# Pooled attention scores over 128 rows, quartered loads, an early gather and later weight halves in a fused attention, expert and Mish kernel

## The chip, the cores and the metric

The kernel runs on one core of a Trainium2 chip. The metric is device time in microseconds of one execution, the median of the runs. The core has TensorE (matmul), VectorE, ScalarE, GpSimd and SyncE (SP), which issues the kernel's direct transfers; 16 DMA engines move the data.

## The reference

Three stages follow one another; shapes are those of the kernel.

```python
# attention: 2 batches, 8 heads, 576 positions, width 64
q_d, k_d, v_d = (t.reshape(2, 8, 144, 4, 64).mean(axis=3) for t in (q, k, v))
out_up = np.repeat(softmax(q_d @ k_d.T / 8) @ v_d, 4, axis=2)
out_local = softmax(where(abs(i - j) < 4, q @ k.T / 8, -1e9)) @ v
x = (out_up + out_local) as [1152, 512]
# 8 experts, top 1, capacity 288
e = argmax(x @ w_gate); g = softmax(x @ w_gate)[e]
y = g * (relu(x @ w1[e]) @ w2[e])      # w1 512 x 1024, w2 1024 x 512, rows over capacity are 0
# dense layer with Mish; w_in and w_out are float64
h = y @ w_in                           # 512 x 2048
out = (h * tanh(log1p(exp(h)))) @ w_out
```

The pooled scores, `q_d @ k_d.T`, are the part that the change computes in another way.

## The kernel before

**Attention** runs in steps `t`. At each step one unit starts its scores (`units[t].scores()`), the unit before it takes its exponentials, the one three steps back is transposed (`turn`) and the one four steps back is multiplied by the values. A unit is a `Local` (four heads of one tile of 96 rows, with its window of 102 keys; 12 tiles, two units each) or a `Down` (two heads of one half, 72 rows, of the pooled attention of one batch; 16 units). `ORDER` fixes the sequence: six local units, six pairs of a pooled and a local one, ten pooled ones in a row (steps 18 to 27), twelve local ones. The second batch's pooled units start at step 20.

Heads stand in pairs on the 128 partitions: 64 rows are one head, 64 the other (`a` = 0 or 1). A pooled unit takes its head's 64 rows of the pooled queries `qd` and keys `kd` (L484 to L499). Ahead of its two score matmuls it issues zero matmuls (`beat(s.sc, 2)`, L328): 128 x 512 in bfloat16, whose result the scores overwrite. Pooling (`pool_qk`, L452) sums four neighbours, on VectorE by one reduction or on GpSimd by three additions; the table `sums` says at which step VectorE pools which pair, and `before(t)` what GpSimd pools.

`before(t)` (L821) also issues loads: constants at step 6 (`load_consts`), and behind them all four loads of the second batch's keys and queries (`load_qk`); at step 8 `turn_consts` (VectorE copies of the constants) and the second batch's `v4` loads with their pools; at the steps in `CLEAR` one of nine clears of the DRAM grid; expert weights from step 22 (`load_pre`, eight pieces) and four halves of the float64 weights (`load_half`). All these transfers stand in SP's queue in the order in which they are issued, together with each tile's `vt` and `vw` loads and the `up` loads.

Up to step 37 the framework orders each engine's instructions by their priorities and its own estimate of time; from then on TensorE follows the program's order (`in_order`).

**The end of attention.** Each token gets an expert and a row (`Route`: `choose`, `place`), is scaled by its gate and scattered into the grid (`send`). The first expert's rows do not wait for the last three tiles: `gather(i)` (L891) multiplies tile 9, 10 or 11 by a one-hot matrix of rows, and `grid_rows` (L901) transposes what the grid already holds; VectorE adds the two (L1079). `gather(EARLY)` (tile 9) stands at step `END` = 44; tile 10's stood just ahead of `grid_rows` and `gather(11)`, once tile 11 is placed. `place` issues as many zero matmuls ahead of its rank matmuls (L730 to L732) as `WAITS` says: 6 for tile 10, 3 for tile 11.

**Experts** (L1272 on) run in 32 steps: eight experts with 192, 192, 184, 168, 160, 152, 144 and 120 rows (`CAPS`), four steps each. A step is `first` (L1214, 16 matmul instructions) and the `second` of the step before (L1229, 16 instructions); each uses one piece of 512 KB out of a ring of eight (`RING`), and `fetch()` loads the next piece into the place that came free, four steps ahead. In the same steps the float64 weights are split into two fp32r parts: `conv_steps(c)` makes `split` of half `c-1`, `round` of half `c`, `clamp` of half `c+1` (for this kernel a look by ScalarE, L263 and L264) and loads halves up to `c + AHEAD` (L252). Halves are 512 KB; eight are loaded before the experts start, halves 28 to 31 after them.

**The dense layer** multiplies three column blocks of 384 tokens by the split weights (`up`, L1331; `out`, L1399).

Of the kernel before, what the change touches and what calls it, by code (L numbers as in the profile page):

```python
# [9 lines left out]
F32 = mybir.dt.float32  # L10
# [27 lines left out]
CLEAR = (11, 12, 13, 14, 17, 18, 19, 23, 24)  # L38
# [5 lines left out]
AHEAD = 8  # L44
# [39 lines left out]
WAITS = {10: 6, 11: 3}  # L84
# [220 lines left out]
def attention(ctx, k, pre):  # L305
# [35 lines left out]
    def load_qk(b, s0, s1):  # L341
        for which, src in ((1, io["kT"]), (0, io["qT"])):
            for h in range(2):
                out = qkt[b][which][h][:, :, s0:s1]
                nc.sync.dma_start(out=out, in_=src[b, :, 2 * h : 2 * h + 2, s0:s1])
# [101 lines left out]
    def pool_new(b):  # L447
        qd = rot.tile([128, HP, SD], F32, tag="qd", name=f"qd{b}")
        kd = rot.tile([128, HP, SD], F32, tag="kd", name=f"kd{b}")
        down[b] = (qd, kd)  # L450

    def pool_qk(b, hp, which, eng):  # L452

        d, x = down[b][which][:, hp, :], qkt[b][which][hp // 2][:, hp % 2, :]
        x = x.rearrange("p (s r) -> p s r", r=4)
        if eng is nc.vector:
            nc.vector.reduce_sum(d, x, axis=AX.X)
        else:
            nc.gpsimd.tensor_add(d, x[:, :, 0], x[:, :, 1])
            nc.gpsimd.tensor_add(d, d, x[:, :, 2])  # L460
            nc.gpsimd.tensor_add(d, d, x[:, :, 3])
        if which == 0:
            eng.tensor_scalar_mul(d, d, 1.0 / 128.0)

# [14 lines left out]
    class Down:  # L479
# [6 lines left out]
        def scores(s):  # L486
            qd, kd = down[s.b]
            s.sc = bank("sc", "dsc" + s.nm, 3)
            beat(s.sc, 2)
            for j in range(2):  # L490
                r = slice(64 * s.a, 64 * s.a + 64)
                nc.tensor.matmul(  # L492
                    s.sc[:HALF, j * SD : (j + 1) * SD],
                    qd[r, s.hp + j, s.hf * HALF : s.hf * HALF + HALF],
                    kd[r, s.hp + j, :],
                    start=(j == 0),
                    stop=(j == 1),
                    skip_group_check=True,
                )  # L499
# [322 lines left out]
    def before(t):  # L822
# [8 lines left out]
        if t == 6:  # L831
            load_consts()
            load_qk(1, 0, S)
            for hp in range(HP):
                pool_qk(1, hp, 1, gps)
        if t == 8:
            turn_consts()
            load_v4(1, 0)
# [77 lines left out]
    while t < END or ready or choosing or chosen or placing or gating:  # L916
# [30 lines left out]
        if t == END:  # L947
            xt.extend(bank("tp", f"x0{c}", 2) for c in range(2))
            gather(EARLY)
# [31 lines left out]
        if NTT - 1 in sends:  # L981
            for i in range(EARLY + 1, NTT - 1):
                gather(i)
# [105 lines left out]
def moe(ctx, k, full, pre):  # L1089
# [63 lines left out]
    with ExitStack() as c1:  # L1153
# [107 lines left out]
        load_to(AHEAD - 1)  # L1261
# [256 lines left out]
```

## Time and profile before

| what | value |
|---|---|
| median of 3 runs | 487.97 us (487.36 to 554.25) |
| the profiled execution, own time | 489.28 us |
| its span, first to last instruction | 487.5 us |
| mean granted TensorE clock | 0.993 |
| attention, experts, dense layer (by TensorE's first matmul of each) | 0 to 128, 128 to 277, 277 to 487.5 us |

The page names engines PE (TensorE matmul), PEld (TensorE weight load), DVE (VectorE), ACT (ScalarE), POOL (GpSimd) and SP. A row of the timeline gives the start, the length, the engine, the line, the operation, the tile written and read with its shape, the count of instructions put together, and in brackets the idle time before with what ended it. An fp32 matmul appears as two instructions. The lengths of matmuls contain their pipeline's end, so the time that one takes from the stream is read from the starts of its neighbours. The chain of waits is the work that ended last, followed back from the last instruction.

### The profile page before, as it was taken

Reading aid. Unit: us, or ns where it says so; the run is one execution under the profiler, and the core shown is the slowest. Engines: PE = TensorE matmul, PEld = TensorE weight load, DVE = VectorE, ACT = ScalarE, POOL = GpSimd, SP = SyncE. Lnnn points to the kernel's source line nnn. Section 1 sums busy time; section 2 is a strip of 40 time slices with the busy share of each in tenths; the row PEclk is TensorE's granted clock in tenths of the full one; section 3 lists DMA queues with packets and bytes.
Section 4 is the critical chain, followed back from the end, with each engine's and each line's share of the span. In section 5 each row is a group of like instructions: output and inputs, shape, how many; then the busy total and the mean of one; then the engine's idle time right before and its main releaser. Section 6 shows DMA issues by size and latency. Waiting matters only on the chain.

```text
span 487.5 us, 8749 instructions
## 1 busy us (share of the span) xinstructions
PE 469.3 (96%) x3136; PEld 424.1 (87%) x3151; DVE 362.8 (74%) x738; ACT 245.0 (50%) x564; POOL 169.8 (35%) x158
## 2 busy tenths in 40 slices
PE   8989999998999999999899999999999999999992
PEld 4767777887899999999899999999888999999982
DVE  2776666769888777688789069999897878687780
ACT  2534545666545555665574156546354454544441
POOL 0364730635376466787665100223320000200002
PEclk9999999999999999999999999999999999999997
DMA  8787989867399999999988130000010000100001
GB/s 243 189 280 197 286 252 336 299 216 243 130 317 287 313 305 332 316 335 289 326 291 310 63 112 0 1 0 1 1 67 1 0 1 0 67 0 1 1 2 70
DMA packets 36205, 78.96 MB, mean 162 GB/s; under 512 B 4829, under 2 KB 17853, under 8 KB 35865
## 3 DMA queue, kind: packets, MB, share of 16 engines
q1 hardware_dynamic: 34281, 73.59, 47.5%
q0 software_dynamic: 1872, 4.73, 2.8%
q8 instruction: 27, 0.44, 0.4%
q14 instruction: 25, 0.20, 0.1%
HBM read 68.26 MB, written 10.04 MB: 161 GB/s over the span
## 4 chain that ended last, share of the span: by engine, by line
PE 48%; issue 28%; DMA 10%; DVE 9%; POOL 2%; ACT 0%; SPq 0%; POOLq 0%; DVEq 0%
PE hlm L1214 11%; PE yam L1229 11%; PE h2m L1331 4%; PE sc L596 4%; DMA mw250r<-in_w 3%; DMA mw153r<-in_w 3%; DMA xgm<-grid 2%; DMA pack<-in_c_pack 2%; PE pv L644 2%; POOL out L149 2%; PE dsc L492 2%; PE dpv L532 2%; PE oam L1399 2%; PE tp L629 1%; PE sc L605 1%
## 5 line engine op out<-in xcount | busy, mean ns | idle before, releaser
L1331 PE MATMUL h2m<-mxh,mw 128*128 128x384 f32 x384 | 103.0, 338 | 0.0
L1399 PE MATMUL oam<-mw,gm 128*128 128x512 f32 x432 | 102.6, 390 | 0.0
L1399 PEld LDWEIGHTS oam<-mw,gm 128*128 128x128 f32 x432 | 80.7, 188 | 15.0
L1331 PEld LDWEIGHTS h2m<-mxh,mw 128*128 128x128 f32 x384 | 70.1, 187 | 1.1
L1331 PE MATMUL h2m<-mxl,mw 128*128 128x384 f32 x192 | 64.9, 338 | 0.0
L149 POOL DMA_INDIRECT out<-obm,tok_s x9 | 8.9, 988 | 121.6 <-ACT obm L1410 121.3
L296 POOL TENSOR_TENSOR mw_in_t<-mw_in_t 128x512 f32<-128x512 f32 x16 | 22.3, 1392 | 56.9 <-DVE mw_in_t L293 51.1
L1387 ACT CAST gm<-wtm 128x768 fp32r<-128x768 f32 (+1 forms) x26 | 20.3, 784 | 36.3 <-DVE wtm L1386 36.2
L1331 PEld LDWEIGHTS h2m<-mxl,mw 128*128 128x128 f32 x192 | 36.0, 187 | 1.0
L1381 ACT ACTIVATE um<-wtm,two 128x768 f32<-128x768 f32 (+1 forms) x26 | 23.0, 888 | 25.3 <-DVE wtm L1379 25.2
L1369 ACT ACTIVATE um<-h2m 128x768 f32<-128x768 f32 (+1 forms) x26 | 19.6, 761 | 28.8 <-PE h2m L1331 28.8
L1378 DVE TENSOR_SCALAR um<-um 128x768 f32<-128x768 f32 (+1 forms) x26 | 13.5, 526 | 25.9 <-ACT um L1369 25.9
L296 POOL TENSOR_TENSOR mw_out_t<-mw_out_t 128x512 f32<-128x512 f32 x16 | 25.1, 1567 | 18.8 <-DVE mw_out_t L293 18.8
L618 ACT ACTIVATE p<-sc,mx 96x102 f32<-96x102 f32 (+1 forms) x96 | 25.0, 340 | 13.0 <-DVE mx L612 9.1
L1384 DVE SCALAR_TENSOR_TENSOR wtm<-wtm,um 128x768 f32<-128x768 f32 (+1 forms) x26 | 23.3, 895 | 8.9 <-ACT um L1383 8.4
L1388 DVE TENSOR_TENSOR gm<-wtm,gm 128x768 fp32r<-128x768 f32 (+1 forms) x26 | 25.2, 976 | 5.7 <-ACT gm L1387 5.7
L302 POOL TENSOR_TENSOR mw<-mw_in_t,mw 128x512 fp32r<-128x512 f32 x16 | 21.5, 1345 | 19.1 <-ACT mw L301 16.3
L286 DVE TENSOR_SCALAR mw_out_t<-mr 128x512 int32<-128x512 int32 x16 | 17.5, 1091 | 13.4 <-POOL mw L302 11.0
L692 POOL TENSOR_TENSOR x<-x,up 96x512 f32<-96x512 f32 x12 | 15.2, 1270 | 35.1 <-DMA up<-up_d 13.5
L302 POOL TENSOR_TENSOR mw<-mw_out_t,mw 128x512 fp32r<-128x512 f32 x16 | 21.3, 1332 | 16.9 <-ACT mw L301 12.8
L596 PEld LDWEIGHTS sc<-kt,qt 64*96 64x96 f32 x192 | 18.3, 159 | 7.8 <-issue 7.3
L1385 DVE SCALAR_TENSOR_TENSOR um<-wtm,um 128x768 f32<-128x768 f32 (+1 forms) x26 | 24.4, 937 | 0.5
(304 smaller groups left out, 1070.9 us busy)
## 6 DMA issues: line engine op xcount, KB each, us to landing
mr<-in_w_in SPq DMA_DIRECT2D x16, 512.0 KB
mr<-in_w_out SPq DMA_DIRECT2D x16, 512.0 KB
grid<-zero SPq DMA_DIRECT2D x9, 512.0 KB
pr<-in_w SPq DMA_DIRECT2D x8, 512.0 KB
vt<-in_vt SPq DMA_DIRECT2D x12, 204.0 KB
up<-up_d SPq DMA_DIRECT2D x12, 195.0 KB
v<-in_v SPq DMA_DIRECT2D x4, 576.0 KB
vw<-in_vw SPq DMA_DIRECT2D x8, 232.7 KB
```

The source lines that it names most:

```text
L296: s.k.nc.gpsimd.tensor_add(b, b, a)
L302: s.k.nc.gpsimd.tensor_sub(s.w[:, 1, :], s.b, s.w[:, 0, :].bitcast(F32))
L596: nc.tensor.matmul(sc[:TP, j * w : (j + 1) * w], qt[j // 2][r, j % 2, t0 : t0 + TP], kt[j // 2][r, j % 2, k0 : k0 + w], start=(j == 0), st ...
L618: nc.scalar.activation(s.p[:, h, :w], s.sc[:TP, h * w : (h + 1) * w], AF.Exp, bias=s.mx[:, h : h + 1], scale=0.125,)
L1214: nc.tensor.matmul(hl[:, fi, :n], w1[:, kk : kk + 128], xe[:, c, :n], start=(c == 0), stop=(c == 3))
L1229: nc.tensor.matmul(ya[q][d // 2][:, (d % 2) * 256 : (d % 2) * 256 + n], w2[:, kk : kk + 128], h[:, fi, :n], start=(f + fi + d % 2 == 0), s ...
L1331: nc.tensor.matmul(hp[:, fi, :CH], wi[kk // 512][:, a, kk % 512 : kk % 512 + 128], xs[b][:, c, :], start=(c == 0 and a + b == 0), stop=(c ...
L1381: nc.scalar.activation(u, w, AF.Ln, bias=k.two)
L1384: vec.scalar_tensor_tensor(out=w, in0=w, scalar=2.0, in1=u, op0=ALU.add, op1=ALU.mult)
L1385: vec.scalar_tensor_tensor(out=u, in0=w, scalar=2.0, in1=u, op0=ALU.subtract, op1=ALU.mult)
L1388: vec.tensor_sub(g[:, :, 1, :], w, g[:, :, 0, :].bitcast(F32))
L1399: nc.tensor.matmul(o, g[t][:, fi, a, :], wo[fi][:, b, :], start=(f == 0 and fi == 0 and a + b == 0), stop=(f == 7 and fi == 1 and a == 1),)
```

## The change

Five edits. Pooled scores: the pooled keys of each pair of heads are kept twice, once with the lower 64 rows only and zeros above (`kd[0]`), once with the upper 64 rows and zeros below (`kd[1]`); ScalarE copies the upper rows over, and the pooling engine then zeroes them in the first. The two score matmuls go over all 128 rows, with one zero matmul ahead instead of two. Loads: the second batch's keys and queries come in quarters, one at each of steps 7 to 10, their pools on GpSimd at steps 9 and 10, `v4` and the rest at step 11, and the grid clears at steps 13 to 21. The gather of tile 10 goes to step `END`, behind that of tile 9. The three zero matmuls ahead of tile 11's rank matmuls go. Float64 halves are loaded four steps ahead instead of eight; the first eight stay as they were.

```diff
--- before.py
+++ after.py
@@ -35,13 +35,13 @@
 PACK = 2 * TP + 4 * E + NTT + 3 * E + NTT * NTT + CUT
 EARLY = 9
 STEPS = 5
-CLEAR = (11, 12, 13, 14, 17, 18, 19, 23, 24)
+CLEAR = (13, 14, 15, 16, 17, 18, 19, 20, 21)
 DUE0 = 2
 UP0 = 3
 PRE = 22
 RING = 8
 FIRST_C = 24
-AHEAD = 8
+AHEAD = 4
 LATE = 28
 CONV = {2: 28, 3: 29, 4: 30, 6: 31, 7: 32}
 IN_SEQ = 8
@@ -81,7 +81,7 @@
 TURN = {40: (37,), 41: (38,), 42: (39,)}
 VALS = {40: (36,), 41: (37,), 42: (38,), 43: (39,)}
 SPINS = {42: 1}
-WAITS = {10: 6, 11: 3}
+WAITS = {10: 6}
 ALL = 42
 DIRECTLY = 37
 ORDER = "LLLLLL" + "DL" * 6 + "D" * 10 + "L" * 12
@@ -338,9 +338,10 @@
     woken = one.tile([128, 1], BF16, name="woken")
     nc.scalar.activation(woken, wake[:, :1], AF.Exp)
 
-    def load_qk(b, s0, s1):
-        for which, src in ((1, io["kT"]), (0, io["qT"])):
-            for h in range(2):
+    def load_qk(b, s0, s1, only=(1, 0), hs=(0, 1)):
+        for which in only:
+            src = io["kT" if which else "qT"]
+            for h in hs:
                 out = qkt[b][which][h][:, :, s0:s1]
                 nc.sync.dma_start(out=out, in_=src[b, :, 2 * h : 2 * h + 2, s0:s1])
 
@@ -446,12 +447,15 @@
 
     def pool_new(b):
         qd = rot.tile([128, HP, SD], F32, tag="qd", name=f"qd{b}")
-        kd = rot.tile([128, HP, SD], F32, tag="kd", name=f"kd{b}")
+
+        kd = [rot.tile([128, HP, SD], F32, tag=f"kd{a}", name=f"kd{b}{a}") for a in range(2)]
+        gps.memset(kd[1][:64], 0.0)
         down[b] = (qd, kd)
 
     def pool_qk(b, hp, which, eng):
 
-        d, x = down[b][which][:, hp, :], qkt[b][which][hp // 2][:, hp % 2, :]
+        d, x = down[b][which], qkt[b][which][hp // 2][:, hp % 2, :]
+        d = (d[0] if which else d)[:, hp, :]
         x = x.rearrange("p (s r) -> p s r", r=4)
         if eng is nc.vector:
             nc.vector.reduce_sum(d, x, axis=AX.X)
@@ -461,6 +465,9 @@
             nc.gpsimd.tensor_add(d, d, x[:, :, 3])
         if which == 0:
             eng.tensor_scalar_mul(d, d, 1.0 / 128.0)
+        else:
+            nc.scalar.copy(down[b][1][1][64:, hp, :], d[64:])
+            eng.memset(d[64:], 0.0)
 
     def pool_v(b, hf):
         v4 = v4s[b, hf]
@@ -486,13 +493,12 @@
         def scores(s):
             qd, kd = down[s.b]
             s.sc = bank("sc", "dsc" + s.nm, 3)
-            beat(s.sc, 2)
+            beat(s.sc, 1)
             for j in range(2):
-                r = slice(64 * s.a, 64 * s.a + 64)
                 nc.tensor.matmul(
                     s.sc[:HALF, j * SD : (j + 1) * SD],
-                    qd[r, s.hp + j, s.hf * HALF : s.hf * HALF + HALF],
-                    kd[r, s.hp + j, :],
+                    qd[:, s.hp + j, s.hf * HALF : s.hf * HALF + HALF],
+                    kd[s.a][:, s.hp + j, :],
                     start=(j == 0),
                     stop=(j == 1),
                     skip_group_check=True,
@@ -830,11 +836,15 @@
             pool_v(0, 1)
         if t == 6:
             load_consts()
-            load_qk(1, 0, S)
-            for hp in range(HP):
-                pool_qk(1, hp, 1, gps)
         if t == 8:
             turn_consts()
+        if 7 <= t < 11:
+
+            load_qk(1, 0, S, ((t < 9) * 1,), ((t - 7) % 2,))
+        if t in (9, 10):
+            pool_qk(1, 2 * t - 18, 1, gps)
+            pool_qk(1, 2 * t - 17, 1, gps)
+        if t == 11:
             load_v4(1, 0)
             load_v4(1, 1)
             pool_v(1, 0)
@@ -946,7 +956,8 @@
         del gating[: len(sends)]
         if t == END:
             xt.extend(bank("tp", f"x0{c}", 2) for c in range(2))
-            gather(EARLY)
+            for i in range(EARLY, NTT - 1):
+                gather(i)
         streams = []
         for u, n in zip(us or [None], [new] + [[]] * len(us)):
             streams.append(urgent(k, finish(u, n), P_LAST if u is units[-1] else P_VALUES if t >= FREE else 0))
@@ -979,8 +990,6 @@
             sends += [i for i in gating if i not in held]
             gating[:] = held
         if NTT - 1 in sends:
-            for i in range(EARLY + 1, NTT - 1):
-                gather(i)
             grid_rows()
             gather(NTT - 1)
         for i in sends:
@@ -1258,7 +1267,7 @@
             turn_x(0)
         else:
             xes[0] = k.xe0
-        load_to(AHEAD - 1)
+        load_to(IN_SEQ - 1)
         halves[0].clamp()
         c = 0
         for i, (q, f) in enumerate(steps):
```

## Rows read from the trace of the kernel before

**Rows 1.** The page: busy time by engine, and the granted clock in 40 slices.

```profile
PE 469.3 (96%) x3136; PEld 424.1 (87%) x3151; DVE 362.8 (74%) x738; ACT 245.0 (50%) x564; POOL 169.8 (35%) x158
...
PEclk9999999999999999999999999999999999999997
```

**Rows 2.** Timeline, 62 to 66 us: start, length, engine, line, tile, idle before.

```profile
62.25 0.40 ACT L523 COPY dpt<-dtp 72x288 f32<-72x288 f32 x1 [1.16 <-PE dtp L519]
...
62.68 0.60 PE L330 MATMUL dsc<-idle 128*128 128x512 bf16 x2
...
63.20 0.45 PEld L492 LDWEIGHTS dsc<-kd,qd 64*72 64x72 f32 x4 [0.42 <-issue]
63.20 0.71 PE L492 MATMUL dsc<-kd,qd 64*72 64x144 f32 x4
...
63.84 0.44 PE L519 MATMUL dtp<-ident,dp 72*72 72x72 f32 x4
...
64.12 0.75 PEld L532 LDWEIGHTS dpv<-vd,dpt 72*72 72x72 f32 x8
64.34 0.68 PE L532 MATMUL dpv<-vd,dpt 72*72 72x65 f32 x8
...
65.38 0.71 PE L492 MATMUL dsc<-kd,qd 64*72 64x144 f32 x4
```

**Rows 3.** Chain of waits, in order of time: an fp32 stream of 192 columns.

```profile
133.61 2.60 PE yam L1229 x16
```

**Rows 4.** End of attention: chain (gather), then the timeline, 122 to 128 us.

```profile
124.48 1.41 PE x L895 x8
...
122.27 0.37 DVE L761 TENSOR_SCALAR one_hot<-pack,row,gate 96x192 f32<-96x192 f32 x1
...
124.27 0.17 PE L731 MATMUL pp<-ohb,tri 96*96 96x8 bf16 x1 [0.66 <-DVE ohb L719]
...
124.91 0.38 DVE L761 TENSOR_SCALAR one_hot<-pack,row,gate 96x192 f32<-96x192 f32 x1
...
126.42 1.55 PE L895 MATMUL x<-one_hot,x 96*128 96x192 f32 x8
```

**Rows 5.** Timeline of TensorE's weight loads, 231 to 242 us, idle before in brackets.

```profile
231.09 2.11 PEld L1214 LDWEIGHTS hlm<-xem,mw151r 128*128 128x128 f32 x16 [0.52 <-PE yam L1229]
...
236.26 2.11 PEld L1214 LDWEIGHTS hlm<-xem,mw152r 128*128 128x128 f32 x16 [1.00 <-PE yam L1229]
...
241.71 2.11 PEld L1214 LDWEIGHTS hlm<-xem,mw153r 128*128 128x128 f32 x16 [0.68 <-issue]
```

**Rows 6.** Transfers of weights: chain (length is issue to landing), then SP's issues.

```profile
216.49 12.56 DMA mw250r<-in_w
...
229.17 12.43 DMA mw153r<-in_w
...
217.55 0.33 SPq L221 DMA_DIRECT2D mw151r<-in_w  x1
...
229.17 0.33 SPq L221 DMA_DIRECT2D mw153r<-in_w  x1
```

**Rows 7.** Windows of 5 us: engines' busy time, granted clock, DMA share, GB/s.

```profile
145.00:150.00 5.00, 5.00 (x33) 5.00 (x32) 4.86 (x4) 2.35 (x7) 3.79 (x3) 1.00 0.81 227
...
230.00:235.00 5.00, 4.69 (x37) 4.48 (x36) 4.90 (x5) 3.18 (x8) 4.19 (x4) 1.00 1.04 302
235.00:240.00 5.00, 4.20 (x33) 4.00 (x33) 4.90 (x5) 2.44 (x6) 3.37 (x3) 1.00 1.02 259
240.00:245.00 5.00, 4.43 (x39) 4.32 (x38) 2.58 (x4) 3.02 (x8) 2.50 (x2) 1.00 1.01 409
245.00:250.00 5.00, 5.00 (x42) 5.00 (x41) 4.86 (x6) 2.77 (x7) 2.81 (x3) 1.00 1.04 316
```

**Rows 8.** Timeline, 16 to 36 us: what waited for early loads.

```profile
25.49 0.94 PE L373 MATMUL tp<-wz,vt 128*102 128x80 f32 x8 [1.30 <-DMA vt<-in_vt]
...
31.33 0.21 DVE L435 CAST tri<-pack 96x96 bf16<-96x96 f32 x1 [2.73 <-DMA pack<-in_c_pack]
```

## The prediction, made before the changed kernel was run

> **What bounds the kernel now.** I read the page's busy shares and its clock line first [rows 1]: TensorE is busy 96% of the span, and the granted clock is in its top tenth in all but the last slice (1.00, which is 2.4 GHz, in each window of [rows 7]). So the time is the length of TensorE's own instruction stream plus the few places where it waits, and each edit counts only as far as it shortens the stream or moves a wait. The timeline of the pooled units [rows 2] shows how one step is built: zero matmuls from 62.68 us, two score matmuls (four instructions, since each fp32 matmul is two) from 63.20, transposes from 63.84, a zero matmul from 64.12, values from 64.34, next scores at 65.38. That is 2.18 us a step, filled by TensorE's own stream. The reader should see one thing more: the weight load of the values starts at 64.12, 0.22 us before their first matmul and under the zero matmul; that of the scores starts in the same instant as its matmul, after 0.42 us of idle. The scores are the instructions over 64 rows; the switch into and out of them is not overlapped.
>
> Then the experts. At 145 to 150 us TensorE is busy 5.00 us of 5 [rows 7]; from 231 us three waits stand ahead of the first-layer weight loads, 0.52, 1.00 and 0.68 us [rows 5], and the chain goes through two weight transfers that take 12.56 and 12.43 us from issue to landing [rows 6]. The windows say why: the DMA share is over 1 from 230 to 250 us, against 0.81 at 145 to 150 [rows 7]. So the late experts are bound by transfers, the early ones are not. Last, the end of attention is a chain between VectorE and TensorE [rows 4].
>
> **Pooled scores, 16 units.** A zero matmul goes: 64.12 to 64.34 is 0.22 us [rows 2]. The scores over 128 rows: the row nearest in kind is a full-row fp32 stream, 16 instructions of 192 columns in 2.60 us, 0.846 ns a column and instruction [rows 3]; 144 columns by 4 instructions are 0.49 us, where 63.20 to 63.84 is 0.64. The gap ahead goes too: two zero matmuls from 62.68 end at 63.12, and the scores start at 63.20, 0.08 later. Together 0.22 + 0.15 + 0.08 = 0.45 us a unit. Bounds: 0.22 if nothing but the zero matmul goes, 0.45 if the whole exposed part goes. I take 0.45, since the row of the values shows a full-row load hidden in just this place.
>
> The Trainium skill, "TensorEngine Tiling (Array Packing)", Key Properties, says that changing the tiling mode drains the engine; the rows agree (0.42 us without a load, 0.08 us without a matmul). Against this, "TensorE: Matmul & The Clock Gate", "Why this matters for your kernels", says that a single matmul over few rows takes the same time as one over 128; by that alone only the 0.22 us would go, and this result is a rival below.
>
> How many of the 16 count? The first two stand ahead of transfers: at 25.49 us TensorE had waited 1.30 us for a vt load, and at 31.33 VectorE had waited 2.73 us for the constants [rows 8]. Both were issued before anything that the change moves, so reaching them sooner only lengthens the wait. The other 14: 14 x 0.45 = 6.3 us. In the ten units in a row 2.18 us becomes 1.73, and I assume that no other engine and nothing in the local units behind them takes it back.
>
> **What it adds there.** Per pooled key pair one ScalarE copy and one memset of 64 x 144 (8 pairs), and two memsets of the zero half at the start. The nearest copy, 72 x 288, takes 0.40 us [rows 2], so 8 cost at most 3.2 us of ScalarE, beside other work. The memset waits for ScalarE's copy, and VectorE's (or GpSimd's) next instructions stand behind it: for the four pairs of the first batch, at steps 3 to 7, from 0 to about 1 us each, what ScalarE has queued. I take 0: this falls ahead of the waits at 25.5 and 31.3 us, which hide it. Without that cover it is up to 2 us.
>
> **The loads of the second batch** go from one block at step 6 to quarters at steps 7 to 10, v4 and its pools from step 8 to 11, and grid clears from 11 to 24 into 13 to 21. On SP, vt and vw loads come ahead of a part of them. The two waits in [rows 8] stay, being on earlier issues; bounds are a gain of 1.5 us (the constants land sooner with less beside them) and a loss of 1.5 (a query quarter issued at step 9 is late for VectorE's pool at step 13, with scores and routing queued behind it). I take 0.
>
> **Tile 10 gathered early.** Before, its 8 instructions (1.41 us in the chain) stood between the last rank matmul and the grid transposes. Its one-hot is made at 122.27 + 0.37 = 122.64, when TensorE is on the three zero matmuls that are removed as well, and then waits 0.66 us until 124.27 [rows 4]. So it fits: 122.7 + 1.41 = 124.1. The transposes come 1.41 us sooner, and the last gather follows them or tile 11's one-hot (124.91 + 0.38 = 125.29) instead of 126.42. Gain 1.0 us; at worst, when the grid rows land late, 0.2.
>
> **Halves four ahead.** No half is loaded in expert steps 0 to 3, where the share is 0.81 [rows 7] and TensorE waits for nothing: no gain there. All 20 move four steps later, so steps 20 to 23, the expert with 152 rows, get one each that they had not. Price: from the landing of mw250r (229.05) to that of mw153r (241.60) the queue delivered what was issued from 217.55 to 229.17 [rows 6], seven pieces of 0.524 MB and 0.29 MB of rows, 3.96 MB in 12.55 us, 316 GB/s. Four halves are 6.6 us of transfer. A step of this expert is two layers of 16 x 152 x 0.846 ns = 2.06 us [rows 3] and a fourth of the turn's eight transposes (four take 0.28 us, [rows 2]), 4.26 us; its two pieces and rows, 1.12 MB, take 3.55. The room is 4 x 0.71 = 2.8 us. The rest, 3.8 us, becomes waiting, as the ring of eight pieces is already late when it starts (2.2 us of waits, [rows 5]). Bounds: at the mean of 409 and 316 GB/s [rows 7] a step with a half (1.64 MB) takes 4.53 us, and four cost 1.1; at the mean of 302 and 259, 5.86 and 6.4. Below nothing: the whole 2.2 us of waits could go, if they came from the halves of steps 0 to 3. I take 3.8.
>
> **Sum.** -6.3 - 1.0 + 3.8 = -3.5 us. The profiled execution took 489.28 us (span 487.5), so 485.8; it is 1.3 above the median shown, 487.97. Against the median: 484.5 us.
>
> **Rivals.**
> - The late halves cost nothing (0.25). Speaks for it: 409 GB/s in one window. Against: 259 in another, with a share over 1 in both. Time: 487.97 - 7.3 = 480.7, or 479 with the constants landing sooner. The Trainium skill, "DMA: Bandwidth & Descriptors", Specifications, gives about 358 GB/s from HBM for a core; by that the sum is an estimated cost near 1 us. The measured 316 decides for me.
> - The full-row scores save only the zero matmul (0.12): 14 x 0.22 = 3.1 instead of 6.3, 487.7 us. The row of the weight loads speaks against it.
> - Slower (0.13): transfers become the bound earlier, at steps 16 to 23, and each half is now due three steps after its issue, 13 us, when a transfer takes 12.5. ScalarE's look at a half then waits, and the ReLU queued behind it holds TensorE. At 300 GB/s two pieces, a half and rows (1.64 MB) take 5.5 us, against steps of about 4.5 and 4.3: 4 x 1.0 + 4 x 1.2 = 8.8 us. With -7.3 that is 489.5, up to 491 when a late look adds to it. It decides from a rate under about 305 GB/s over these eight steps.
> - One zero matmul less lets the clock fall to 1.2 GHz among the pooled units (0.04): ten steps of 1.73 us would take twice that, 17 us more, about 501 us. TensorE has no pause there [rows 2], so I hold it unlikely.
>
> **How the numbers follow.** My forecast has 0.46 (482 to 487 us). The range 479 to 490 reaches to the free halves below and most of the slower rival above. Within 2% (9.8 us, about what a measurement of this kernel can tell from no change) lie all cases but the clock and what adds gains that I set to 0: faster 0.06, same 0.89, slower 0.05.
>
> **What would show it.** Right: pooled steps of about 1.7 us, score weight loads starting under the zero matmul, scores four instructions in 0.5 us; the last gather about 1 us after the last rank matmul instead of 2.1; weight waits on TensorE from expert step 20 on adding up to about 6 us instead of 2.2. Wrong: pooled steps over 1.95 us; a ScalarE or VectorE wait between the pools and scores before 60 us that is new; no weight waits after 225 us; a clock row under 1.00 before the last slice.

## The result, and the profile after

The changed kernel took 497.34 us (median of 4 runs, 494.61 to 499.34) beside 489.1 of the kernel before (median of 4, one of them 554.25). The ratio on record, formed from comparable runs, is 1.014, interval 1.009 to 1.019; the two medians as they stand divide to 1.017. The forecast was 484.5 us; the time lies above its range. (In most series some runs, the 554.25 us among them, are longer by 1.5 to 16% at a lower clock: the ratios and the medians of time, clock and work below are without them, but the profiled executions of e1, e2, e3, e6, e12 and e13 are of that kind.) The profiled execution took 499.34 us, 10.06 more than that of before.

The page of the changed kernel, busy time and clock, as in [rows 1]:

```profile
PE 471.9 (95%) x3117; PEld 433.5 (87%) x3132; DVE 358.8 (72%) x742; ACT 247.7 (50%) x572; POOL 172.0 (35%) x164
...
PEclk9995799998899999999999999999999999999998
```

TensorE has 19 fewer records (the 16 and 3 zero matmuls) and yet more busy time. The clock line says why: slices 4 and 5 (37 to 62 us) and 10 and 11 (112 to 137 us) are below the top tenth, where before only the last slice was. A ladder of equal places in the two traces shows where the 10 us arise.

| place (start, us) | before | after | difference |
|---|---|---|---|
| scores of the 8th pooled unit | 56.61 | 66.64 | +10.03 |
| scores of the 16th | 74.83 | 80.92 | +6.09 |
| first matmul behind the pause in the routing | 113.19 | 119.19 | +6.00 |
| first expert matmul | 128.09 | 135.87 | +7.78 |
| first long block of the dense layer | 279.96 | 289.91 | +9.95 |
| span | 487.5 | 497.6 | +10.1 |

**The pooled steps did what was forecast.** Between the 8th and the 16th the change wins 3.94 us in eight steps, 0.49 a step. The timeline of the changed kernel, answering to [rows 2]:

```profile
69.86 0.38 PE L330 MATMUL dsc<-idle 128*128 128x512 bf16 x1
69.87 0.61 PEld L498 LDWEIGHTS dsc<-kd,qd 128*72 128x72 f32 x4
70.08 0.65 PE L498 MATMUL dsc<-kd,qd 128*72 128x144 f32 x4
...
70.57 0.41 PE L525 MATMUL dtp<-ident,dp 72*72 72x72 f32 x4
```

The weight load starts at 69.87 under the zero matmul, and 70.08 to 70.57 is 0.49 us, where it was 0.64. By the Trainium skill, "TensorEngine Tiling (Array Packing)", Key Properties, a change of mode drains the engine; the 0.49 in place of 0.64 agrees, though no row shows the drain itself. The Trainium skill's other rule that the prediction names, in "TensorE: Matmul & The Clock Gate", "Why this matters for your kernels", is that a matmul over few rows takes as long as one over 128. By it only the 0.22 us of the zero matmul would have gone; the 0.49 a step, and e6 below, do not agree with that.

**What was lost, was lost ahead of them.** The timeline of the changed kernel, 29 to 45 us (idle time before an instruction, and what ended it, in brackets):

```profile
32.23 0.44 POOL L463 TENSOR_TENSOR kd<-kt 128x144 f32<-128x144 f32 x1 [4.00 <-DMA kt<-in_kT]
...
33.98 0.31 ACT L469 COPY kd<-kd 64x144 f32<-64x144 f32 x1 [5.75 <-POOL kd L465]
...
36.38 0.31 ACT L469 COPY kd<-kd 64x144 f32<-64x144 f32 x1 [2.10 <-POOL kd L465]
36.72 0.65 ACT L513 ACTIVATE dp<-dsc,dmx 72x144 f32<-72x144 f32 x2
...
37.26 0.39 ACT L529 COPY dpt<-dtp 72x288 f32<-72x288 f32 x1
...
37.79 1.20 PE L538 MATMUL dpv<-vd,dpt 72*72 72x65 f32 x8 [4.80 <-ACT dpt L529]
39.03 0.16 DVE L548 TENSOR_SCALAR drec<-dpv 72x2 f32<-72x2 f32 x1 [5.14 <-PE dpv L538]
...
41.62 0.31 ACT L469 COPY kd<-kd 64x144 f32<-64x144 f32 x1 [2.10 <-POOL kd L465]
...
43.52 1.60 PE L650 MATMUL pv<-vw,pt 102*96 102x96 f32 x8 [1.52 <-ACT vw L641]
```

Read it upward from 37.79: TensorE waits 4.80 us for `dpt`, a ScalarE copy of a first-batch unit. That copy took 0.39 us and waited for nothing of its own; it stood in ScalarE's queue behind the new copy of the second batch's keys. The new copy waits for GpSimd's pool (5.75 us), and the pool for the keys' DMA (4.00 us), issued at 23.16 us. Four such copies, for pairs whose first scores are at 68 us, hold ScalarE for 11.5 us in all (the sum of their four waits). The 1.52 us at 43.52 stand behind the last of them, at 41.62. The Trainium skill, "Perfetto Trace Analysis", Tensor Engine Instruction (MATMUL, LD_WEIGHTS), says that ScalarE, VectorE and GpSimd execute strictly in order; the rows agree, to the 5.75 us.

**And then the clock.** Windows of the changed kernel (columns as in [rows 7], here of 10 us):

```profile
30.00:40.00 10.00, 3.94 (x29) 3.09 (x29) 4.32 (x17) 1.85 (x6) 5.44 (x13) 0.79 0.93 247
40.00:50.00 10.00, 8.12 (x43) 6.94 (x44) 2.65 (x10) 4.63 (x17) 3.67 (x7) 0.50 0.60 154
50.00:60.00 10.00, 9.94 (x71) 8.86 (x71) 5.35 (x16) 3.25 (x12) 9.28 (x14) 0.69 0.63 186
60.00:70.00 10.00, 9.94 (x109) 9.13 (x108) 6.53 (x26) 6.17 (x22) 0.25 (x1) 1.00 0.74 220
```

A mean of 0.79 is 4.2 us at 1.2 GHz out of ten, 0.50 all ten, 0.69 6.2: together 20.4 us at half speed, from within the wait of 4.80 on. The +10.03 as an estimate: TensorE's four waits before 45 us (0.65, 1.26, 4.80, 1.52) add up to 8.23 against 2.15 before, +6.1; of the 20.4 us some 3.6 were waiting, and half of the rest is +8.4; seven units' saving is -3.2. That is 11.3, where 10.03 was measured.

Two smaller losses follow. Between 119 and 136 us the clock falls again (below), and the expert stage is 154.0 us long where it was 151.9. The waits of TensorE's loads for expert weights, answering to [rows 5] and [rows 6], in timeline and chain of the changed kernel:

```profile
243.22 2.11 PEld L1223 LDWEIGHTS hlm<-xem,mw152r 128*128 128x128 f32 x16 [0.78 <-PE yam L1238]
249.46 2.10 PEld L1223 LDWEIGHTS hlm<-xem,mw153r 128*128 128x128 f32 x16 [1.48 <-ACT hm L1227]
...
263.29 2.01 PEld L1223 LDWEIGHTS hlm<-xe,mw162r 128*128 128x128 f32 x16 [1.56 <-issue]
```

```profile
225.07 12.47 DMA mw151r<-in_w
237.62 13.01 DMA mr<-in_w_out
250.75 12.43 DMA mw162r<-in_w
```

The first two are 2.26 us together, as the 2.20 of before. The third is new: it stands one expert later, at the one with 144 rows, and ends as `mw162r` lands, 12.43 us after its issue at 250.75. With it and 0.19 us at the next piece the waits are 4.0 us, 1.8 more than before, which is most of the stage's 2.1. The transfers take 12.4 to 13.0 us, as before.

**The tail.** Timeline of the changed kernel, 118 to 136 us, answering to [rows 4], then its window from 120 us, and last the row of the kernel before at the same pause:

```profile
119.19 0.16 PE L736 MATMUL pp<-capb,ones 1*96 1x8 bf16 x1 [1.22 <-DVE rt L753]
...
133.18 0.86 PE L918 MATMUL gt<-ident,xg 96*128 96x96 f32 x8
...
134.27 1.54 PE L905 MATMUL x<-one_hot,x 96*128 96x192 f32 x8 [0.22 <-DVE one_hot L767]
```

```profile
120.00:130.00 10.00, 9.95 (x63) 8.70 (x63) 8.27 (x55) 5.12 (x17) 4.77 (x6) 0.66 0.62 213
```

```profile
113.19 0.16 PE L730 MATMUL pp<-capb,ones 1*96 1x8 bf16 x1 [1.18 <-DVE rt L747]
```

The grid transposes now stand right behind the last rank matmuls and the last gather follows its one-hot, as forecast. But from 121 us on the clock was at 1.2 GHz for 6.8 us (0.66 in the window 120 to 130). The pause ahead of it, 1.22 us, was there before too (1.18) and no fall followed. Of the four runs, two had a mean clock of 0.975 (494.6 and 495.9 us), the others 0.967 and 0.968 (498.8 and 499.3); the profiled one is that of 499.3.

### The profile page after: what moved, and what is told of

It is laid out like the page before. It is cut to its first block, busy times and chain, and to the rows that moved or that the text cites. A ratio compares the mean times of both kernels' runs of the same rounds, so it can differ in the third digit from the quotient of the medians.

```text
span 497.6 us, 8722 instructions
## 1 busy us (share of the span) xinstructions
PE 471.9 (95%) x3117; PEld 433.5 (87%) x3132; DVE 358.8 (72%) x742; ACT 247.7 (50%) x572; POOL 172.0 (35%) x164
## 4 chain that ended last, share of the span: by engine, by line
PE 46%; issue 27%; DMA 13%; DVE 7%; POOL 3%; ACT 1%; SPq 1%; POOLq 0%; DVEq 0%
PE hlm L1223 11%; PE yam L1238 11%; PE h2m L1340 4%; PE pv L650 3%; PE sc L602 3%; DMA v<-in_v 3%; DMA mr<-in_w_out 3%; DMA mw151r<-in_w 3%; DMA mw162r<-in_w 2%; PE dpv L538 2%; POOL out L149 2%; DMA kt<-in_kT 2%; PE oam L1408 2%; PE dsc L498 2%; PE tp L635 1%
## 5 line engine op out<-in xcount | busy, mean ns | idle before, releaser
L602 PEld LDWEIGHTS sc<-kt,qt 64*96 64x96 f32 x192 | 19.7, 169 | 8.2 <-issue 7.7
L602 PE MATMUL sc<-kt,qt 64*96 64x102 f32 (+1 forms) x192 | 24.2, 268 | 1.5 <-issue 0.7
L650 PE MATMUL pv<-vw,pt 102*96 102x96 f32 (+1 forms) x192 | 23.4, 274 | 1.5 <-ACT vw L641 1.5
```

Of the source, the lines that this page charges most:

```text
L602: nc.tensor.matmul(sc[:TP, j * w : (j + 1) * w], qt[j // 2][r, j % 2, t0 : t0 + TP], kt[j // 2][r, j % 2, k0 : k0 + w], start=(j == 0), st ...
L650: nc.tensor.matmul(pv[:TP, h * VC : h * VC + n], s.pt[:w, h * TP : (h + 1) * TP], v[:w, o : o + n], start=True, stop=True, skip_group_chec ...
```

## The experiments

One more quantity helps to read them. A run of T us that spends t of them at 1.2 GHz has a mean clock of 1 - t/(2T); where TensorE bounds it, the low stretch cost t/2. So time times mean clock estimates what the run would take at 2.4 GHz throughout; I call it the **work**. The kernel before has 485.9 us of it in its profiled execution and medians of 486.2 to 487.2 on the chips of the experiments, the changed kernel 482.9 (mean of four). By that estimate the change saves 3 to 4 us of work and pays some 11 to 12 us in clock. The estimate has a bias: time that TensorE waits at 1.2 GHz is counted as if it were work at half speed, so a kernel with a low clock in its waits shows too little work (by up to 1.8 us here, half of the 3.6 us that were waiting).

**First: which part did it?** Theory A: the ScalarE copies for the second batch. Rival B: the later, quartered loads as such. In e1 GpSimd copies for the second batch; in e2 the loads have their old order, and ScalarE still copies.

```diff
 e1
-            nc.scalar.copy(down[b][1][1][64:, hp, :], d[64:])
+            (nc.scalar.copy if b == 0 else nc.gpsimd.tensor_copy)(down[b][1][1][64:, hp, :], d[64:])
 e2
+            load_qk(1, 0, S)
+            for hp in range(HP):
+                pool_qk(1, hp, 1, gps)
         if t == 8:
             turn_consts()
-        if 7 <= t < 11:
-            load_qk(1, 0, S, ((t < 9) * 1,), ((t - 7) % 2,))
-        if t in (9, 10):
...
```

> The changed kernel, but the upper rows of the second batch's pooled keys are copied by GpSimd, which pools them, and not by ScalarE. Theory A (ScalarE's copies stand in its queue ahead of the first batch's exponentials and wait there for keys that are still being loaded, so TensorE stands still, and the clock falls after that): the 4.8 us wait of TensorE at 33 to 38 us goes, the granted clock stays at 1.00 up to 100 us, and what is left is the shorter pooled stream (-6), the early gather (0 to -1) and the later halves (+2.2): 484.5 us, 482 to 487. Rival B (the quartered loads bring the keys late, whoever copies them): the wait and the low clock stay, about 497 us. Rival C (one zero matmul less and full rows let the clock fall by themselves): no wait, but a stretch at 1.2 GHz before 60 us, 491 us or more.

> The changed kernel with the second batch's loads, pools and the grid clears where they were before (one block at step 6, v4 at step 8). ScalarE still copies. Theory A: worse than the changed kernel, since all four copies of the second batch now stand in ScalarE's queue earlier, ahead of a local unit's exponentials, and the keys land no earlier than in the kernel before (about 32.7 us, pooled until 39): TensorE waits 10 us or more between 22 and 40 us, the clock falls, about 505 us (500 to 512). Rival B (the quarters are the cause): the wait goes, 484 to 488 us.

e1: 0.998 (0.992 to 1.003); the changed kernel's 1.4% is gone, and so is the wait of 4.80 us: TensorE's longest between 20 and 60 us is 1.80, for a `vt`. The saving that theory A forecast (484.5 beside 488, 0.993) is not shown, and the clock was not at 1.00 up to 100 us: in the profile it falls behind that `vt`, and behind a wait of 3.88 us at 72.89. e2: 1.021 (1.010 to 1.033), worse than the change, though less than the forecast (505 beside 488, 1.035). The timeline of e2 shows the queue at its plainest:

```profile
34.87 0.31 ACT L469 COPY kd<-kd 64x144 f32<-64x144 f32 x1 [13.56 <-POOL kd L465]
...
43.86 1.56 PE L650 MATMUL pv<-vw,pt 102*96 102x96 f32 x8 [17.71 <-ACT pt L639]
```

With the old order the copies are put into ScalarE's queue earlier, at step 6, and TensorE stands 17.71 us. A is right about the cause of the loss, B falls: the quartered loads make the stall shorter, not longer.

**The wait and the clock apart.** e4 is the changed kernel with 24 zero matmuls instead of one ahead of the values that waited, so that TensorE works through the wait (their result is overwritten).

```diff
-            beat(pv, 1)
+            beat(pv, 24 if now_t[0] == 10 else 1)
```

> The changed kernel with 24 zero matmuls (5.2 us) instead of one ahead of the value matmuls that wait for ScalarE at step 10, so that TensorE is not idle there. Splits the wait from the clock. Theory A: the first value matmul starts as late as before (about 38 us), but the granted clock stays at 1.00 from there on, the 20.5 us at 1.2 GHz go, and with them some 7 to 8 us: about 489 us (486 to 492). If the clock falls for another reason than this wait, it falls all the same, and the time stays at 495 to 499 us.

Windows of e4:

```profile
30.00:40.00 10.00, 8.22 (x54) 4.87 (x54) 4.59 (x20) 1.85 (x6) 5.40 (x13) 1.00 0.95 249
40.00:50.00 10.00, 7.35 (x58) 6.21 (x58) 3.40 (x12) 4.98 (x18) 3.61 (x7) 0.83 0.64 164
50.00:60.00 10.00, 9.79 (x100) 8.80 (x101) 8.95 (x29) 5.70 (x21) 9.28 (x14) 1.00 0.88 263
```

The low stretch shrank from 20.4 us to 3.4 (0.83 in one window), behind the next wait, 2.50 us at 43.58. The mean clock rose to 0.983. The ratio is 1.008 (1.003 to 1.012), against 1.014; the forecast, 489 beside 488, was 1.002. The two intervals overlap and come from different series of runs. That the clock carries a part is shown by the windows and not by the ratios; how large a part stays open.

**The halves.** e3 is the changed kernel with eight ahead, e8 the kernel before with four, e7 is e1 with eight (`AHEAD`; in e8 also `load_to(IN_SEQ - 1)`, as in the change). b0 is the kernel before itself, for a second profile.

```diff
 e3, e7
-AHEAD = 4
+AHEAD = 8
 e8
-AHEAD = 8
+AHEAD = 4
```

> The changed kernel with the halves eight ahead, as before. If the later halves are what the expert stage lost (289.91 - 135.87 = 154.0 us from its first matmul to the dense layer's first full run, against 279.96 - 128.09 = 151.9): that stage takes 151.9 us again and the time is 2.2 us less than the changed kernel's, about 495 us. If the stage is longer for another reason (its start after a low clock, other traffic), it stays at 154 us.

> The kernel before with one edit: the halves of the float64 matrix are asked for four joined transfers ahead in place of eight. By the recorded prediction (a half's landing costs what the shorter lead doesn't cover) +3.8 us, a ratio of 1.008, and the expert stage (first hlm to the last h2m matmul) 3.8 us longer than that of a kernel with eight ahead on the same chip. By the present theory (the stage is bound by the bytes, whichever lead the issues have; with eight ahead it took 157 us too in other runs) 1.000, within 0.997 to 1.003.

> The changed kernel with GpSimd's copies and with the halves eight ahead: pooled scores, quartered loads, early gather without the three zero matmuls. Theory A: as the one-zero-matmul version of this series, less up to 1 us for the gather: ratio 0.985. If the three zero matmuls ahead of tile 11's rank matmuls, or the quarters, cost something, it is slower than that version by 1 us or more. Against the version with GpSimd's copies and halves four ahead (0.998 in the series before): if the later halves cost 2 us or more, it lies that much lower.

> The kernel before, run on the chip of this series for its trace. Ratio 1.00. If the transfers of this chip are slower than those of the first trace, its expert stage takes 154 to 156 us instead of 151.9 with eight halves ahead too; if the later halves were what made that stage long in the runs so far (154.0, 155.9 to 156.9), it takes 152.

e3: 1.008 (1.003 to 1.014), against 1.014 of the changed kernel with four; the intervals overlap. As e3 is the changed kernel but for the halves and ran on the chip of e1, it also says what the copies cost there: 1.008 against 0.998. e7: 1.000 (0.997 to 1.003), where e1 with four had 0.998. e8: 1.003 (0.999 to 1.007), which excludes 1.008. b0: 1.001 (0.998 to 1.005). The chain of e8 and then that of e10 (eight ahead, same chip), first expert matmul and first long block of the dense layer:

```profile
125.81 5.52 PE hlm L1214 x32
...
283.71 15.56 PE h2m L1331 x88
```

```profile
124.72 5.52 PE hlm L1219 x32
...
282.93 15.56 PE h2m L1336 x88
```

That is 157.9 us with four ahead and 158.2 with eight. By the same two rows the stage took 151.9 to 160.0 us in the twelve profiles with eight (before 151.9, e12 153.9, e14 153.9, e11 154.0, e3 155.9, e15 156.1, e5 157.1, e7 157.4, b0 157.6, e10 158.2, e6 and e13 160.0) and 154.0 to 159.1 in the five with four (after 154.0, e1 156.6, e4 156.9, e8 157.9, e2 159.1). It differs by 8 us between executions of one setting, so a cost of the halves up to about 3 us (e8's interval) is not excluded, and none is shown in the time.

The waits do show something. In each of the five profiles with four ahead TensorE's weight loads wait at the expert with 144 rows, 0.9 to 1.75 us in all (1.56 and 0.19 in the changed kernel, 0.81 and 0.30 in e8); in none of the twelve with eight ahead is there a wait over 0.15 us at that expert. So the later halves do delay weights, as the prediction had it, but one expert later and by less than its 3.8 us.

**The pooled scores alone.** e5 is the kernel before with the full-row scores, GpSimd copies for the second batch, and one zero matmul; e6 keeps both; e14 is the kernel before with nothing but one zero matmul less.

```diff
 e5 and e14 (e6 without this)
-            beat(s.sc, 2)
+            beat(s.sc, 1)
```

> The kernel before with the pooled scores over 128 rows and one zero matmul less, nothing else; the second batch's upper rows are copied by GpSimd. Theory A: no wait of TensorE on ScalarE before 40 us; 0.45 us less in each of at least 14 units, 6.3 us less, ratio 0.987. Rival C (with less zero work the clock falls at pauses that it passed before): its mean granted clock lies under that of the two-zero-matmul version of this series by 0.003 or more, and the gain is eaten, ratio 0.993 to 1.005.

> The same with the two zero matmuls kept. If the switch between 64 and 128 rows costs what the starts of the neighbouring instructions show (0.15 + 0.08 us a unit), 14 x 0.23 = 3.2 us less than before: ratio 0.993. If a matmul over 64 rows simply takes as long as one over 128, ratio 1.000. Rival C: as fast as the version with one zero matmul or faster, with the higher clock.

> The kernel before with one edit: one zero matmul ahead of the pooled scores in place of two; scores over 64 rows, loads, gather and halves as before. My rival 'only the zero matmul' gives 14 x 0.22 = 3.1 us, a ratio of 0.994. If the switch into 64 rows takes until then anyway (the zero matmul ran under it), 0.998 to 1.000. If the zero matmul is what holds the clock, the mean granted clock falls from 0.994 to below 0.985 and the ratio lies over 1.000, though nothing else is changed.

e6: 0.994 (0.990 to 0.998), forecast 0.993. e14: 0.9945 (0.989 to 1.0004, from three runs), forecast 0.994; by itself that is not clear of no change. The profiles settle it: from the 8th to the 16th pooled unit a step is 2.28 us in the kernel before, 2.06 in e14, 2.00 in e6 and 1.79 in the changed kernel. So the zero matmul is worth 0.22 us and the switch 0.28, and together they make the 0.49. e5 has two runs to compare (486.9 and 489.7 us), so it has no interval; it should have had both parts together, about 0.994 x 0.9945 = 0.989, and its work is only 2.8 us below that of before. The timeline of e5 shows one reason:

```profile
65.69 0.16 DVE L685 TENSOR_TENSOR lga<-lga,up 96x8 f32<-96x8 f32 x1 [4.76 <-DMA up<-up_d]
...
66.89 0.53 PE L330 MATMUL dpv<-idle 128*128 128x512 bf16 x1 [1.76 <-DVE od L553]
```

The pooled outputs go to DRAM and come back as `up` rows. With short steps VectorE reaches their first use before the transfer lands, waits 4.76 us, and TensorE 1.76 behind it. Before, that transfer was covered by the steps' length. e7 shows the same for the second batch's query pools on GpSimd, in its timeline:

```profile
58.91 0.47 PE L498 MATMUL dsc<-kd,qd 128*72 128x144 f32 x2 [1.11 <-POOL qd L467]
...
61.24 0.47 PE L498 MATMUL dsc<-kd,qd 128*72 128x144 f32 x2 [1.87 <-POOL qd L467]
```

The join of the `up` rows held TensorE there too, 1.99 us at 73.09.

**The loads alone.** e10 is the kernel before with the changed kernel's quartered loads, later pools and clears, but scores over 64 rows.

> The kernel before with the second batch's loads in quarters and their later order as in the changed kernel, but with the scores left in two row groups of 64, so that no ScalarE copy exists. Theory: what hurt was the copy in ScalarE's queue and not the later transfers, and with steps of 2.2 us GpSimd has the time to make the pools: 1.000 (0.996 to 1.004), no idle time over 1.5 us of TensorE between 30 and 45 us. Rival: the later transfers alone delay the second batch's pools past their scores: TensorE waits on POOL qd or kd by 2 us or more in the second batch, and the ratio is over 1.005.

1.000 (0.995 to 1.004), clock 0.994 as before, no wait of TensorE over 0.7 us between 18 and 125 us. So in steps of 2.18 us the loads cost nothing that shows; in e7's short steps the query pools come late.

**The best of it together.** e11 is e5 with the early gather and with the joins of the `up` rows two steps later; e12 the same with two zero matmuls. e13 is e11 with the two early pauses filled by zero matmuls; e15 is e7 with the later joins and the quarters a step earlier.

```diff
 e11, e12, e15
-DUE0 = 2
+DUE0 = 4
 e15
-        if 7 <= t < 11:
+        if 6 <= t < 10:
...
 e13 (from e11)
+            if s.a == 0 and s.i == 2:
+                beat(tp, 4)
...
-            beat(s.sc, 1)
+            beat(s.sc, 7 if now_t[0] == 10 else 1)
```

> The kernel before with the full-row pooled scores and one zero matmul, the second batch's upper rows copied by GpSimd, the loads whole and in their old order, the early gather of tile 10, eight halves ahead, and the joins of the up rows begun two steps later, so that they don't wait for their transfer. Theory: 14 units save 0.45 to 0.49 us each (6.3 to 6.9 us), the gather 0.9 us, nothing new waits: 480.5 to 482 beside 488 of the kernel before, a ratio of 0.985, if the clock stays as in the kernel before. Rival: steps with one zero matmul hold the clock less well; then falls to 1.2 GHz of 3.4 us or more in the pooled run or behind it take 1.7 us or more each back, and the ratio lies at 0.99 to 1.01.

> The same with both zero matmuls kept. Theory: 14 units save what the switch between the row groups costs, 0.23 us each (3.2 us), the gather 0.9 us: a ratio of 0.990 to 0.992. If the second zero matmul is what holds the clock, this one is no slower than the one with one zero matmul; if it isn't, it is slower than that by 14 x 0.22 = 3.1 us, 0.6%.

> The kernel with one zero matmul that measured 1.006 (full rows, GpSimd copies, early gather, eight ahead, later joins), with four zero matmuls ahead of the third local tile's transposes and six more ahead of the pooled scores of step 10, so that TensorE works instead of pausing before the two transfers it reaches early. Theory: the pauses of 1 to 1.7 us at 24 to 32 us are what the falls to 1.2 GHz at 25 to 42 us follow; filled, the mean granted clock rises from a median of 0.974 to 0.985 or more and the ratio falls to 0.990 to 0.996. Rival: it is the steps with fewer zero matmuls themselves; then the clock stays at 0.974 +- 0.004 and the ratio at 1.006 or, with 10 more zero matmuls of 0.22 us, up to 1.01.

> Full rows with one zero matmul, GpSimd copies, early gather, eight ahead, joins two steps later, and the second batch's quartered loads issued one step earlier than in the changed kernel. Theory: with quarters the constants and vt land sooner (the kernel with quarters alone had no wait for vt or the constants), the query pools are in time, and no wait of TensorE over 1 us is left before 110 us: clock 0.985 or more, ratio 0.985 to 0.990. Rival: the clock falls in the short steps whatever the waits: clock at 0.975, ratio over 1.000.

e11: 1.006 (1.002 to 1.010); e12: 0.999 (0.996 to 1.002); e13: 1.009 (1.004 to 1.014); e15: 0.997 (0.990 to 1.003). All four missed the theory's forecast, e11 and e13 on the wrong side of 1 (e15 has two runs to compare). And e12, with its second zero matmul, is faster than e11, where its expectation had it slower by 0.6% unless that zero matmul holds the clock. Set beside their clocks (medians of clock and work):

| kernel | ratio | median clock | work against before, us |
|---|---|---|---|
| e10, loads | 1.000 | 0.994 | -0.1 |
| e6, full rows, two zero matmuls | 0.994 | 0.994 | -2.1 |
| e14, one zero matmul less | 0.9945 | 0.990 | -3.4 |
| e12, full rows, gather, joins, two | 0.999 | 0.986 | -3.5 |
| e15, e7 with later joins | 0.997 | 0.984 | -5.7 |
| e11, full rows, gather, joins, one | 1.006 | 0.976 | -6.6 |
| e13, e11 with pauses filled | 1.009 | 0.970 | -6.9 |

The saving in the pooled steps is there: 1.79 us a step in e11 as in the changed kernel, and 6.6 us of work against a forecast of 7.2 to 7.8. In the table the more a kernel saves, the lower its clock; but work is time times clock, so a part of that order comes from the estimate's bias. The trace of e11 says where the clock fell, first in its timeline with the row of the kernel before at the same place behind it, then in its windows:

```profile
23.71 0.94 PE L373 MATMUL tp<-wz,vt 128*102 128x80 f32 x8 [0.49 <-DMA vt<-in_vt]
...
31.50 0.47 PE L496 MATMUL dsc<-kd,qd 128*72 128x144 f32 x2 [1.67 <-DVE qd L465]
```

```profile
33.34 0.46 PE L492 MATMUL dsc<-kd,qd 64*72 64x144 f32 x2 [0.85 <-DVE qd L463]
```

```profile
30.00:40.00 10.00, 8.50 (x47) 7.26 (x48) 5.40 (x21) 4.49 (x16) 7.79 (x19) 0.59 0.90 243
40.00:50.00 10.00, 10.00 (x91) 8.71 (x90) 6.87 (x23) 4.23 (x14) 7.08 (x10) 0.90 0.77 237
```

VectorE's pool stands behind the constants [rows 8]. TensorE comes to it earlier than before, waits 1.67 us instead of 0.85, and 10.2 us at 1.2 GHz follow (0.59 and 0.90). The steps between 50 and 71 us, with their one zero matmul, run at 1.00. e13 fills that wait. Timeline and windows of its profiled execution, which took 505.15 us:

```profile
100.44 1.67 PE L373 MATMUL tp<-wz,vt 128*102 128x80 f32 x8 [3.54 <-DMA vt<-in_vt]
```

```profile
30.00:40.00 10.00, 9.91 (x92) 7.85 (x91) 7.35 (x30) 5.45 (x19) 6.08 (x15) 1.00 0.91 261
40.00:50.00 10.00, 10.00 (x103) 8.81 (x103) 8.05 (x25) 4.92 (x17) 6.38 (x12) 1.00 0.63 182
90.00:100.00 10.00, 6.90 (x62) 5.50 (x60) 8.74 (x46) 4.42 (x18) 5.09 (x5) 0.89 0.89 281
100.00:110.00 10.00, 9.56 (x50) 8.06 (x50) 3.54 (x30) 5.84 (x17) 1.91 (x2) 0.50 0.68 201
```

No pause at 31, no fall there, and full clock through the pooled steps of 1.69 us. But now TensorE reaches at 96.9 us the `vt` of tile 9, which it used at 104.4 before, waits 3.54 us, and a longer fall begins. SP issued that load only 1.2 us earlier than before (93.4 against 94.6), behind the `up` rows. So in this execution it is not in the short steps that the clock goes, but at the next transfer that they run into. For the runs whose ratio is given, of 492.8 to 498.6 us, that is not shown: the numbers of e13's rival came out (clock 0.970, ratio 1.009). Against the rival speak e14 with its 0.990, and that the clock also fell in the profiles of e6 and e12, which keep both zero matmuls: for 13.6 us from 91 us on and for 23.9 us from 104 us on. It stays open.

## Why the prediction was wrong, point by point

- **What bounds the kernel** (TensorE's stream and its few waits): right, and the reading that each edit counts by the waits it moves was the right one. I did not apply it to the added copies.
- **Pooled scores, 0.45 us a unit:** right; 0.49 in the profile, and the steps of e6 and e14 show its two parts, 0.28 and 0.22 us. "I assume that no other engine ... takes it back" was wrong for short steps: the `up` rows (1.76 us on TensorE in e5), the query pools (1.11 and 1.87 in e7) and a `vt` (3.54 in e13) were each hidden by the length of the steps before.
- **"What it adds there ... I take 0": the step that failed.** I priced the copies' own time and the memset's wait for a copy, and the waits only for the first batch; these sizes were right (0.31 us a copy, 0.43 a wait of VectorE's memset). I did not ask what the copy itself waits for and what stands behind it. For the second batch it waits for GpSimd's pool and that for a DMA, with first-batch exponentials and copies behind it in ScalarE's queue: 4.80 us of TensorE's time, 1.52 more behind the last copy, and 20.4 us at 1.2 GHz. In place of 0 the copies on ScalarE cost about 1 to 1.6% of the time: e1, without the second batch's, has 0.998, where the changed kernel has 1.014 and e3 1.008; e2 makes it worse. Two of the prediction's signs of being wrong, a new ScalarE wait before 60 us and a clock under 1.00 before the last slice, are this.
- **Loads, 0:** right by themselves (e10: 1.000, 0.995 to 1.004); in short steps a query quarter comes late (e7), the side of the loss that the bounds had named.
- **Tile 10 early, -1.0:** right. From the last mask matmul to the first expert matmul e7 takes 16.35 us (109.52 to 125.87), e5 and e6 without the early gather 17.25 (105.48 to 122.73, 114.56 to 131.81): -0.9. In the changed kernel's own profile the fall of the clock hides it.
- **Halves, +3.8:** the mechanism is there, the size was too large, and its place is wrong. The weight waits forecast as about 6 us instead of 2.2 are 4.0 in the changed kernel, the new ones at the expert with 144 rows and not at that with 152. In time, e8 has 1.003 where 1.008 was forecast, and the stage varies by 8 us without any change. The windows of [rows 7] are of one execution; as a price they were too thin.
- **The clock:** my rival had the right engine and the wrong cause, a zero matmul less among the pooled units, worth 0.04. In the changed kernel the fall starts within the wait of 4.80 us, ahead of them, and its pooled steps from 66 us on run at 1.00; e14 takes just the zero matmul away and keeps 0.990. Most falls follow pauses, and I had called the early waits free because "reaching them sooner only lengthens the wait". In time that held; e11 shows 10.2 us at half speed behind such a wait.

What stays open: whether a pause decides, and which. In the profiles, falls followed, among others, pauses of 1.17 us (e4's tail), 1.22 (the tails of the changed kernel and of e1), 1.40 (e12), 1.67 (e11), 1.74 (e14), 1.80 (e1), 1.87 (e7) and 1.94 (e15). None followed 1.18 and 1.30 us before, 1.72 in e4 or 1.99 in e7, though; and in e11 and e15 the clock was at 1.2 GHz for 3.4 us between 110 and 115 us behind pauses of only 0.25 and 0.56. A pause without a saving, and a saving without a pause, were not both tried. The fastest kernel that is shown is e6, full-row scores with both zero matmuls, 0.6% below the kernel before (0.990 to 0.998).

## What to carry to other kernels

For each instruction that a change adds, write down what it waits for and what stands behind it in its engine's queue, for every place where it is issued; a cheap copy of data needed later belongs on the engine that makes that data, or late in the queue. When steps get shorter, list the transfers whose latency the old length covered: each may become a pause, and on TensorE a pause can cost more in clock afterwards than it lasts. Read the mean granted clock beside every time: time times clock is a first estimate of whether work or clock has changed, to be borne out by the length of a step.

## What the runs showed of the hardware

- The clock fell behind pauses much shorter than the stretch that followed: 10.2 us at 1.2 GHz behind 1.67 us (e11), 20.4 from within a pause of 4.80 on (after).
- The same pause at the end of attention, 1.2 us, was passed at 2.4 GHz in the profiles of before and followed by 6.8 us at 1.2 GHz in that of the changed kernel.
- The expert stage, whose program is the same in all of these kernels but for the order of some loads, took 151.9 to 160.0 us in 17 profiled executions.
- Scores over 64 rows between steps over 128 cost 0.28 us a step more than the same scores over 128 rows with zeros (2.28 against 2.00 us, before and e6).
